# Attention numerators as full 128-row products, with tokens tiled in global pairs

## The chip, the cores and the metric

The kernel runs on one core of a Trainium2 chip. The metric is the device time of one execution in microseconds (us); lower is better. The core's engines are TensorE (PE in the profile, with its weight loads as PEld), VectorE (DVE), ScalarE (ACT), GpSimd (POOL) and SyncE (SP); SP and POOL only start DMA transfers here, apart from a few set-up instructions.

## The reference

Linear attention with cosine weights, followed by a gated feed-forward block (FFN). There are 8 batches, 8 heads, 576 tokens and head size 64; the FFN has model width 512 and inner width 1536.

```python
pos = np.arange(S); theta = np.pi / 2.0 * pos / S
phi(x) = concat([max(x, 0) * cos(theta), max(x, 0) * sin(theta)], -1)
kv  = einsum('bhsf,bhsd->bhfd', phi(k), v)
z   = sum(phi(k), axis=2)
num = einsum('bhsf,bhfd->bhsd', phi(q), kv)
den = einsum('bhsf,bhf->bhs', phi(q), z)[..., None] + 1e-06
x   = (num / den).transpose(0, 2, 1, 3).reshape(B * S, H * D)   # 4608 x 512
out = (silu(x @ w_gate) * (x @ w_val)) @ w_out
```

## The kernel before

**Layout.** The 576 tokens of a batch are cut into NC = 9 chunks of 64 tokens (chunk c holds the tokens 9p + c). Heads are numbered 2g + e; a head's partitions are the half e, and g = 0 to 3 is split into j = g // 2 and i = g % 2. In the transposed queries `qt` the partitions are (i, head dimension), so that 128 partitions hold two heads of 64 rows each.

**Attention of one batch.** `relu_k` (line 166) takes max(k, 0), `vmul` (line 176) multiplies v by the cosine and the sine table, and a 65th column of the table itself gives the denominator. `kv_mm` (line 203) forms the 64 x 130 matrices of all heads in two PSUM banks (cosine part w = 0, sine part w = 1, 65 columns each), and `kv_out` (line 219) copies them to SBUF as `kvs`. The queries are turned by `qturn_pe` (line 194, TensorE transposes, batches 0 and 1) or by `relu_q` and `qturn_dma` (lines 171 and 188, a DMA transpose started by SP, batches 2 to 7).

**The half.** `a_half` (line 242) makes the numerators of four heads for one tile of two chunks: four products with 64 contraction rows each (line 250) into two banks,

```python
lhsT=qt[hs, e, j, c:c + n]                       # 64 rows x 128 tokens
rhs=kvs[hs, e, j]                                # 64 rows x 130 columns
```

then ScalarE scales the cosine part (`tmp`, line 260) and VectorE adds the scaled sine part (`num`, line 262). After both halves (j = 0, 1), `x_norm` (line 267) adds 1e-6, takes the reciprocal and multiplies (line 275, one 128 x 512 product), and `x_turn` (line 281) transposes the tile into `xT`, by TensorE and ScalarE (`fast`) or by a DMA transpose that SP starts (line 295). Tiles never cross a batch or a group of 8 chunks (`tiles_of`, line 232), so each batch has five tiles, one of them with a single chunk: 80 halves in all.

**FFN.** A group is 8 chunks, 512 tokens; there are NTG = 9 groups (0 to 8). `ffn_fc` (line 300) does one of the FC = 12 column blocks: four products for the gate and four for the value (line 312), SiLU on ScalarE (`sg`, line 315), product on VectorE (`ht`, line 317). `ffn_out` (line 322) does one of the group's four output tiles in 12 products (line 329), copies it out of PSUM and writes it with two DMAs (line 344).

**What sets the order.** The schedule is manual: each engine runs its instructions in the order in which the program writes them. PSUM's 8 banks go round in turn (`take`, line 66): a request for two gets the next aligned pair, and banks that are held (the two of `kv_mm`, the output tiles in progress) are skipped. An instruction that gets a bank waits until its last reader is through. From group 1 on, a group is SLOTS = 16 slots, 12 column blocks and 4 output tiles; slot s of group g is 16g + s. After each, the functions that the table `plan` holds for that slot are issued. For batch b from 3 on, `kv_mm` is at slots 1 and 2 of group b - 1, and the ten halves at slots 4 to 13. For batch 2, `relu_q`, `relu_k` and `vmul` are at slots 17 to 20, `qturn_dma` at 20, `kv_mm` at 23 and 24 and the halves at 26 to 35; `qturn_dma` of batch 3 is at 29. Group 2 begins at slot 32. Its first token pair comes from batch 1, the next three from batch 2, the last of them at slots 30 and 31.

Group 0 is special. Its column blocks run in two passes over 256 tokens each, called the a pieces (first 256) and b pieces here; six a pieces come first, with the halves and transposes of tiles 2 and 3 between them (`early`, line 453), then b and a pieces alternate. Its output tiles are done in three pieces of four products for all four tiles (line 470), which holds four banks, with work for batch 1 between them (`sub`, line 411).

Of the kernel before, what the change touches and what calls it, by code (L numbers as in the profile page):

```python
# [9 lines left out]
FP32 = mybir.dt.float32  # L10
# [7 lines left out]
def kernel(  # L18
# [86 lines left out]
    CA = 4  # L105
    load(0, "v", 2)
    load_slots(0, "q", 0, CA)
    load_slots(0, "q", CA, NC)
# [3 lines left out]
    bias = consts.tile([P, 2, 2], FP32)  # L112
    for i, step in enumerate((S, S - 1)):
# [8 lines left out]
    for i, cs in enumerate((csk, cst)):  # L122
        nc.scalar.activation(out=cs[:, :, 0], in_=pos, func=AF.Sin, scale=-rad, bias=bias[:, i, 0:1])
        nc.scalar.activation(out=cs[:, :, 1], in_=pos, func=AF.Sin, scale=rad, bias=bias[:, i, 1:2])
# [94 lines left out]
    def kv_out(b, engs=("act",)):  # L219
        kvs = kvp.tile([P, 2, J, 2 * D1], BF16, name="kvs")  # L220
        ps = st.pop((b, "kvps"))
        held.pop(("kv", b))
        n = 2 // len(engs)
        for i, eng in enumerate(engs):
            es = slice(i * n, (i + 1) * n)
            (nc.scalar.copy if eng == "act" else nc.vector.tensor_copy)(
                out=kvs[:, es].rearrange("p e j x -> p e (j x)"), in_=ps[:, es, 0:J * 2 * D1])
        st[b, "kvs"] = kvs
# [3 lines left out]
    def tiles_of(b):  # L232
        cut = next((g - b * NC for g in range(0, NH + 1, GH) if b * NC < g < (b + 1) * NC), NC)
        res = []
        for lo, hi in ((0, cut), (cut, NC)):
            while lo < hi:
                n = min(2, hi - lo)
                res.append((lo, n))
                lo += n
        return res  # L240

    def a_half(b, c, n, j):

        m = n * SH
        qt, kvs = st[b, "qt"], st[b, "kvs"]
        av = take(2)[0:m, :, 0:4 * D1].rearrange("p i (w e x) -> p i w e x", w=2, e=2)
        for e in range(2):
            for i in range(2):
                hs = slice(i * D, (i + 1) * D)
                nc.tensor.matmul(  # L250
                    out=av[:, i, :, e],
                    lhsT=qt[hs, e, j, c:c + n].rearrange("p c s -> p (c s)"),
                    rhs=kvs[hs, e, j].rearrange("p (w x) -> p w x", w=2),
                    start=True, stop=True,
                )
        if j == 0:
            st[b, "num", c] = smp.tile([P, H, D1], FP32, name="num")
        nv = st[b, "num", c][0:m, 4 * j:4 * j + 4].rearrange("p (i e) x -> p i (e x)", i=2)
        tmp = smp.tile([P, 2, 2 * D1], FP32, name="tmp")
        nc.scalar.activation(out=tmp[0:m], in_=av[:, :, 0].rearrange("p i e x -> p i (e x)"),  # L260
                             func=AF.Copy, scale=cst[0:m, c, 0:1])
        nc.vector.scalar_tensor_tensor(  # L262
            out=nv, in0=av[:, :, 1].rearrange("p i e x -> p i (e x)"), scalar=cst[0:m, c, 1:2], in1=tmp[0:m],
# [3 lines left out]
    def x_norm(b, c, n):  # L267
        m = n * SH
        num = st.pop((b, "num", c))
        den = smp.tile([P, H, 1], FP32, name="den")  # L270
        nc.vector.tensor_single_scalar(out=den[0:m], in_=num[0:m, :, D:D1], scalar=1e-6, op=ALU.add)
        rec = smp.tile([P, H, 1], FP32, name="rec")
        nc.vector.reciprocal(out=rec[0:m], in_=den[0:m])  # L273
        x = xp.tile([P, d_model], BF16, name="x")
        nc.vector.tensor_tensor(  # L275
            out=x[0:m].rearrange("p (h d) -> p h d", h=H),
            in0=num[0:m, :, 0:D], in1=rec[0:m].to_broadcast([m, H, D]), op=ALU.mult,
        )
        st[b, "x", c] = x

    def x_turn(b, c, n, fast=False):
        m = n * SH
        x = st.pop((b, "x", c))
# [235 lines left out]
```

## Time and profile before

| What | Value |
|---|---|
| Median of 3 runs | 363.44 us (363.05 to 364.62) |
| The profiled execution's own time | 362.56 us |
| Its span, first to last instruction | 360.4 us |
| TensorE busy | 329.9 us, 92% of the span |
| VectorE busy | 189.0 us, 52% |
| ScalarE busy | 157.2 us, 44% |
| Line 250, the products of the halves | 320 products, 23.1 us |

The span is what the trace covers; the time of that execution is 2.16 us longer. Busy times of one engine can overlap in the rows of products, since they are pipelined: the start times of successive rows say more than their lengths. An engine's idle time counts only where it delays the chain of work that ends last.

### The profile page before, as it was taken

The page shows a single profiled execution, that of the slowest core. Times are in us where ns is not written, and L with a number is a line of the kernel's source. Part 1 is how long each engine was busy: PE and PEld are TensorE (multiplying, and loading weights), DVE is VectorE, ACT ScalarE, POOL GpSimd, SP SyncE. Part 2 cuts the span into 40 slices and gives each one's busy share as a digit, 9 for nine tenths or more (in the row PEclk, how much of TensorE's full clock was granted, in tenths as well). Part 3 has the DMA queues.
Part 4 walks back from the last instruction along what each step waited for, and adds up shares of the span by engine and source line. Part 5 has one row for each costly group of instructions (what it writes and reads, how often), then busy time and mean ns, then how long its engine had stood idle before and what let it go on. Part 6 is the DMA issues. An engine that isn't in the chain of part 4 may idle for free.

```text
span 360.4 us, 6121 instructions
## 1 busy us (share of the span) xinstructions
PE 329.9 (92%) x2400; PEld 154.0 (43%) x2400; DVE 189.0 (52%) x386; ACT 157.2 (44%) x301; POOL 33.3 (9%) x49
## 2 busy tenths in 40 slices
PE   0678999699956999999999999999999999999994
PEld 0447754244422444444344444444443444444441
DVE  5645753583651787438733874387337544303420
ACT  4544455483721674257425742574245323313311
POOL 8545210002000200020000000000000000000000
PEclk9879999999996999999999999999999999999999
DMA  8999999941962594649460145015501240031013
GB/s 214 196 200 202 206 208 208 256 75 18 217 136 52 88 165 74 144 68 162 81 139 1 25 86 135 6 31 90 129 1 25 57 105 0 1 74 45 0 31 87
DMA packets 56477, 36.39 MB, mean 101 GB/s; under 512 B 30848, under 2 KB 51328, under 8 KB 56448
## 3 DMA queue, kind: packets, MB, share of 16 engines
q0 software_dynamic: 21152, 18.29, 32.1%
q1 hardware_dynamic: 35296, 17.70, 23.2%
q8 instruction: 19, 0.31, 0.4%
q14 instruction: 10, 0.08, 0.1%
HBM read 37.75 MB, written 9.44 MB: 131 GB/s over the span
## 4 chain that ended last, share of the span: by engine, by line
PE 87%; DVE 4%; DMA 3%; SPq 2%; ACT 2%; issue 1%; POOL 0%; ACTq 0%; POOLq 0%
PE banks L312 53%; PE banks L329 25%; PE banks L250 5%; PE banks L212 3%; DMA raw_q<-in_q_dram 2%; DVE x L275 2%; DVE num L262 1%; SPq L189 1%; SPq L344 1%; PE banks L291 1%; PE banks L198 1%; DMA xT<-x 1%; ACT tmp L260 1%; DVE rec L273 0%; ACT xT L293 0%
## 5 line engine op out<-in xcount | busy, mean ns | idle before, releaser
L317 DVE TENSOR_TENSOR ht<-sg,banks 128x512 bf16<-128x512 bf16 (+1 forms) x120 | 75.7, 632 | 98.8 <-PE banks L312 82.7
L312 PE MATMUL banks<-xT,wg_sb 128*128 128x512 bf16 (+1 forms) x480 | 115.3, 363 | 8.8 <-DMA xT<-x 7.0
L312 PE MATMUL banks<-xT,wv_sb 128*128 128x512 bf16 (+1 forms) x480 | 114.5, 361 | 0.0
L315 ACT ACTIVATE sg<-banks 128x512 bf16<-128x512 f32 (+1 forms) x120 | 66.5, 554 | 94.2 <-PE banks L312 93.7
L329 PE MATMUL banks<-wo_sb,ht 128*128 128x512 bf16 x432 | 98.9, 380 | 0.0
L312 PEld LDWEIGHTS <-wv_sb 128*128 128x128 bf16 x480 | 47.5, 99 | 47.5 <-issue 1.1
L312 PEld LDWEIGHTS <-wg_sb 128*128 128x128 bf16 x480 | 42.2, 98 | 49.5 <-DMA xT<-x 7.2
L329 PEld LDWEIGHTS <-ht 128*128 128x128 bf16 x432 | 39.8, 98 | 46.7
L260 ACT ACTIVATE tmp<-banks,cst 128x260 f32<-128x260 f32 (+1 forms) x80 | 37.8, 477 | 42.4 <-PE banks L250 42.4
L262 DVE SCALAR_TENSOR_TENSOR num<-banks,cst,tmp 128x260 f32<-128x260 f32 (+1 forms) x80 | 38.5, 483 | 15.7 <-ACT tmp L260 15.2
L341 DVE COPY ob<-banks 128x512 f32<-128x512 f32 x17 | 11.8, 691 | 37.7 <-PE banks L329 36.2
L275 DVE TENSOR_TENSOR x<-num,rec 128x512 bf16<-128x512 f32 (+1 forms) x40 | 27.6, 690 | 1.4
L341 ACT COPY ob<-banks 128x512 f32<-128x512 f32 x18 | 10.5, 586 | 39.9 <-PE banks L329 39.9
L250 PE MATMUL banks<-kvs,qt 64*128 64x130 bf16 (+1 forms) x320 | 23.1, 227 | 1.1 <-ACT ob L341 0.7
L177 DVE TENSOR_TENSOR v<-raw_v,tab 128x1152 bf16<-128x1152 bf16 x32 | 23.5, 751 | 0.7 <-DMA raw_v<-in_v_dram 0.7
L250 PEld LDWEIGHTS <-qt 64*128 64x128 bf16 (+1 forms) x320 | 9.7, 96 | 32.8 <-issue 30.9
L212 PE MATMUL banks<-v,raw_k 64*64 64x130 bf16 x576 | 12.9, 231 | 8.6 <-DVE v L177 8.6
L212 PEld LDWEIGHTS <-raw_k 64*64 64x64 bf16 x576 | 10.0, 113 | 13.6 <-issue 8.0
L162 ACT ACTIVATE raw_k<-raw_k 128x576 bf16<-128x576 bf16 x24 | 15.8, 675 | 0.0
L162 ACT ACTIVATE r_q<-raw_q 128x576 bf16<-128x576 bf16 x24 | 15.8, 673 | 0.0
L93 POOL DMA_DIRECT2D raw_k<-in_k_dram x7 | 5.2, 743 | 99.9 <-issue 59.3
L291 PE MATMUL banks<-ident,x 128*128 128x128 bf16 (+1 forms) x40 | 4.2, 232 | 6.3 <-DVE x L275 6.3
(38 smaller groups left out, 77.1 us busy)
## 6 DMA issues: line engine op xcount, KB each, us to landing
out_dram<-ob SPq DMA_DIRECT2D x72, 128.0 KB, 2.3
raw_k<-in_k_dram POOLq DMA_DIRECT2D x7, 576.0 KB, 13.0
raw_v<-in_v_dram POOLq DMA_DIRECT2D x6, 576.0 KB, 12.8
raw_q<-in_q_dram POOLq DMA_DIRECT2D x6, 576.0 KB, 12.2
wg_sb<-in_moe_w_gate_dram POOLq DMA_DIRECT2D x6, 256.0 KB, 10.8
wv_sb<-in_moe_w_val_dram POOLq DMA_DIRECT2D x6, 256.0 KB, 11.1
wo_sb<-in_moe_w_out_dram POOLq DMA_DIRECT2D x3, 512.0 KB, 13.0
k<-in_k_dram SPq DMA_DIRECT2D x2, 576.0 KB, 4.2
```

The costliest lines, as they stand in the source:

```text
L162: nc.scalar.activation(out=out, in_=in_, func=AF.Relu)
L177: nc.vector.tensor_tensor(out=v2s[b % 2][:, g, :, :, 0:D], in0=raws[b, "v"][:, g].unsqueeze(2).to_broadcast([P, NC, 2, D]), in1=tab, op=AL ...
L212: nc.tensor.matmul(out=ps[i * D:(i + 1) * D, e, j * 2 * D1:(j + 1) * 2 * D1], lhsT=raws[b, "k"][es, g, c], rhs=v2s[b % 2][es, g, c, :, 0:D ...
L250: nc.tensor.matmul(out=av[:, i, :, e], lhsT=qt[hs, e, j, c:c + n].rearrange("p c s -> p (c s)"), rhs=kvs[hs, e, j].rearrange("p (w x) -> p ...
L260: nc.scalar.activation(out=tmp[0:m], in_=av[:, :, 0].rearrange("p i e x -> p i (e x)"), func=AF.Copy, scale=cst[0:m, c, 0:1])
L262: nc.vector.scalar_tensor_tensor(out=nv, in0=av[:, :, 1].rearrange("p i e x -> p i (e x)"), scalar=cst[0:m, c, 1:2], in1=tmp[0:m], op0=ALU ...
L275: nc.vector.tensor_tensor(out=x[0:m].rearrange("p (h d) -> p h d", h=H), in0=num[0:m, :, 0:D], in1=rec[0:m].to_broadcast([m, H, D]), op=AL ...
L312: nc.tensor.matmul(out=o, lhsT=w[:, kc, fs], rhs=xT[tg][:, kc, ts], start=(kc == 0), stop=(kc == KC - 1))
L315: nc.scalar.activation(out=sg[:, 0:n], in_=ps[0], func=AF.Silu)
L317: nc.vector.tensor_tensor(out=ht[:, fc, r:r + n], in0=sg[:, 0:n], in1=ps[1], op=ALU.mult)
L329: nc.tensor.matmul(out=o_ps[t], lhsT=ht[:, fc, r:r + P], rhs=wo_sb[:, fc], start=(fc == 0), stop=(fc == FC - 1))
L341: (nc.scalar.copy if t % 2 == 0 else nc.vector.tensor_copy)(out=ob, in_=ps)
```

## The change

- `kvs` is replaced by two constant tiles `kvd`, cleared once. `kv_out` writes the two heads of a pair (i = 0, 1) as two copies, one for each half of the partitions and into its own columns, so that a pair's matrices stand on a block diagonal of 128 rows x 260 columns.
- `a_half(t, j)` takes a global tile t = 0 to 35 (chunks 2t and 2t + 1 of the 72). It does two products of 128 rows x 260 columns in place of four of 64 x 130. Tiles 4, 13, 22 and 31 cross from one batch to the next; each of their products is done as two, with 64 tokens each. There are 72 halves.
- `x_norm` multiplies in two products of 128 x 256.
- The tables are written anew: one half per slot. A group's four tiles are at slots 4 to 11 of the group before (group 2's at 20, 21, 23 to 28). Batch 2's key and query work is at slots 16 to 19, its `qturn_dma` at 20, its `kv_mm` at 20 and 21; batch 3's `qturn_dma` is split over 28 and 29. In group 0, tile 2 is issued ahead of the FFN, and the tiles of batch 1 are spread anew.
- The weights' fifth part is loaded ahead of batch 1's keys, and the loads of batches 4 to 7 are issued at three places in the program each.

The diff, cut (constants for the cosine of the ninth chunk, the load order and the unchanged ends of functions left out):

```diff
+    kvd = []
+    for j in range(2):
+        t = consts.tile([P, 2, J, 2, 2, D1], BF16, name=f"kvd_{j}")
+        nc.vector.memset(t, 0.0)
+        kvd.append(t)
...
-    def kv_out(b, engs=("act",)):
-        kvs = kvp.tile([P, 2, J, 2 * D1], BF16, name="kvs")
+    def kv_out(b, engs=("act", "act")):
...
+            hs = slice(i * D, (i + 1) * D)
             (nc.scalar.copy if eng == "act" else nc.vector.tensor_copy)(
-                out=kvs[:, es].rearrange("p e j x -> p e (j x)"), in_=ps[:, es, 0:J * 2 * D1])
+                out=kvd[b % 2][hs, :, :, :, i].rearrange("p e j w x -> p e (j w) x"),
+                in_=ps[hs, :, 0:J * 2 * D1].rearrange("p e (y x) -> p e y x", x=D1))
...
-                    out=av[:, i, :, e],
-                    lhsT=qt[hs, e, j, c:c + n].rearrange("p c s -> p (c s)"),
-                    rhs=kvs[hs, e, j].rearrange("p (w x) -> p w x", w=2),
+                    out=ps[ms, e, 0:4 * D1],
+                    lhsT=st[b, "qt"][:, e, j, c:c + n].rearrange("p c s -> p (c s)"),
+                    rhs=kvd[b % 2][:, e, j].rearrange("p w i x -> p (w i x)"),
...
+    x_turn(0, fast=True)
+    a_(2, 0)()
+    x_turn(1, fast=True)
+    a_(2, 1)()
...
+    at("a0", a_(3, 0))
+    at("a1", a_(3, 1))
+    at("a3", turn(2, True))
+    at("a5", turn(3, True))
...
+    at((0, 0), a_(5, 0), q_(1, 0, 1))
+    at((0, 1), a_(5, 1), q_(1, 1, 1))
+    at((0, 2), turn(4, True), a_(6, 0))
+    at((0, 3), a_(6, 1))
+    at((1, 0), turn(5, True), a_(7, 0))
+    at((1, 1), a_(7, 1))
...
+        keng = "dve" if b == 2 else "act"
+        steps = [lambda b=b, g=g: (relu_k(b, g, g + 1, keng), vmul(b, g)) for g in range(G)]
...
+            fs, tq, tk = [s0 + i // 2 for i in range(8)], (s0 + 4, s0 + 4), (s0 + 4, s0 + 5)
...
+    for t in range(2 * OUT, NTG * OUT):
+        tg, i = divmod(t, OUT)
+        s = SLOTS * (tg - 1) + (4 if tg > 2 or i == 0 else 5) + 2 * i
+        at(s, a_(t, 0))
+        at(s + 1, a_(t, 1), turn(t))
```

How the instructions move, at three places. First SP around the start of group 2; `xT_1053` is group 2's input before and `xT_1120` in the change. Before:

```order
L189 DMA_TRANSPOSE qt_1080<-r_q_1009 128x18x64 x2
L295 DMA_TRANSPOSE xT_1053<-x_1256 128x4x128
L344 DMA out_0_dram<-ob_1273 64x512 x2
L344 DMA out_0_dram<-ob_1301 64x512 x2
L295 DMA_TRANSPOSE xT_1053<-x_1316 128x4x128
L189 DMA_TRANSPOSE qt_1329<-r_q_1231 128x18x64 x2
L344 DMA out_0_dram<-ob_1344 64x512 x2
L344 DMA out_0_dram<-ob_1368 64x512 x2
L295 DMA_TRANSPOSE xT_1053<-x_1383 128x4x128
```

Of the change:

```order
L195 DMA_TRANSPOSE qt_1010<-r_q_955 128x18x64 x2
L290 DMA_TRANSPOSE xT_1120<-x_1117 128x4x128
L290 DMA_TRANSPOSE xT_1120<-x_1176 128x4x128
L290 DMA_TRANSPOSE xT_1120<-x_1219 128x4x128
L339 DMA out_0_dram<-ob_1253 64x512 x2
L195 DMA_TRANSPOSE qt_1257<-r_q_1165 128x18x64
L290 DMA_TRANSPOSE xT_1120<-x_1268 128x4x128
L339 DMA out_0_dram<-ob_1284 64x512 x2
L195 DMA_TRANSPOSE qt_1257<-r_q_1165 128x18x64
L339 DMA out_0_dram<-ob_1301 64x512 x2
```

Group 2's last input tile stood behind the output writes of all four tiles of group 1; it now stands behind those of the first, and behind one of batch 3's two query transposes.

Second VectorE at the start of group 0, from the second tile's `den` on (`ht` is the first FFN result). Before:

```order
L271 TENSOR_SCALAR den_302<-num_291 128x8
L273 RECIPROCAL rec_304<-den_302 128x8
L275 TENSOR_TENSOR x_306<-num_291,rec_304 128x512
L317 TENSOR_TENSOR ht_135<-sg_349,banks_90 128x256
L262 SCALAR_TENSOR_TENSOR num_356<-banks_90,cst_114,tmp_357 128x260
L317 TENSOR_TENSOR ht_135<-sg_368,banks_90 128x256
L262 SCALAR_TENSOR_TENSOR num_356<-banks_90,cst_114,tmp_375 128x260
L271 TENSOR_SCALAR den_378<-num_356 128x8
L273 RECIPROCAL rec_380<-den_378 128x8
L275 TENSOR_TENSOR x_382<-num_356,rec_380 128x512
```

Of the change:

```order
L265 TENSOR_SCALAR den_304<-num_295 128x8
L267 RECIPROCAL rec_306<-den_304 128x8
L271 TENSOR_TENSOR x_308<-num_295,rec_306 128x2x2x64 x2
L257 SCALAR_TENSOR_TENSOR num_341<-banks_90,cst_118,tmp_342 128x260
L257 SCALAR_TENSOR_TENSOR num_341<-banks_90,cst_118,tmp_352 128x260
L265 TENSOR_SCALAR den_355<-num_341 128x8
L267 RECIPROCAL rec_357<-den_355 128x8
L271 TENSOR_TENSOR x_359<-num_341,rec_357 128x2x2x64 x2
L312 TENSOR_TENSOR ht_145<-sg_370,banks_90 128x256
L257 SCALAR_TENSOR_TENSOR num_375<-banks_90,cst_118,tmp_376 128x260
L312 TENSOR_TENSOR ht_145<-sg_387,banks_90 128x256
```

The third tile's `num`, `den`, `rec` and `x` stood between and behind the first two `ht`; they are now ahead of them.

Third ScalarE at the first column blocks of group 1, where batch 2's keys and queries are prepared. Before:

```order
L315 ACTIVATE sg_987<-banks_90 128x512
L260 ACTIVATE tmp_995<-banks_90,cst_114 128x260
L315 ACTIVATE sg_1006<-banks_90 128x512
L162 ACTIVATE r_q_1009<-raw_q_163 128x9x64 x2
L260 ACTIVATE tmp_1016<-banks_90,cst_114 128x260
L315 ACTIVATE sg_1033<-banks_90 128x512
```

Of the change:

```order
L310 ACTIVATE sg_950<-banks_90 128x512
L168 ACTIVATE raw_k_169<-raw_k_169 128x576
L168 ACTIVATE r_q_955<-raw_q_173 128x9x64
L310 ACTIVATE sg_965<-banks_90 128x512
L168 ACTIVATE raw_k_169<-raw_k_169 128x576
L168 ACTIVATE r_q_955<-raw_q_173 128x9x64
```

Each of the first four slots now has one key step and one query step on ScalarE, and the halves of batch 1's last tile have moved out of the first two.

## Rows read from the trace of the kernel before

**Rows 1.** The profile's page: TensorE's busy time, its granted clock in 40 slices.

```profile
PE 329.9 (92%) x2400; PEld 154.0 (43%) x2400; DVE 189.0 (52%) x386; ACT 157.2 (44%) x301; POOL 33.3 (9%) x49
...
PEclk9879999999996999999999999999999999999999
```

**Rows 2.** Waits of TensorE: who waited for whom; us in total, times, longest.

```profile
PE banks L312 <- DMA xT<-x: 7.0, 1, 7.0
PE banks L291 <- DVE x L275: 6.3, 7, 1.9
```

**Rows 3.** Timeline, group 1's end, TensorE and VectorE: start us, length us, engine, line.

```profile
103.81 0.29 PE L250 MATMUL banks<-kvs,qt 64*128 64x130 bf16 x4
105.62 0.69 DVE L275 TENSOR_TENSOR x<-num,rec 128x512 bf16<-128x512 f32 x1
```

**Rows 4.** The chain that ended last, entry of group 2: start us, length us, what.

```profile
108.62 2.45 DMA xT<-x
...
111.12 3.58 PE banks L312 x8
```

**Rows 5.** The same chain in group 4, and in the last two groups.

```profile
200.29 1.83 PE banks L312 x8
202.12 0.23 PE banks L250 x4
...
293.53 20.72 PE banks L312 x96
314.25 10.36 PE banks L329 x48
```

**Rows 6.** Timeline of TensorE, a half and a full-height transpose between output products.

```profile
54.49 0.29 PE L250 MATMUL banks<-kvs,qt 64*128 64x130 bf16 x4
54.71 1.04 PE L329 MATMUL banks<-wo_sb,ht 128*128 128x512 bf16 x4
55.59 0.39 PE L291 MATMUL banks<-ident,x 128*128 128x128 bf16 x4
55.81 1.03 PE L329 MATMUL banks<-wo_sb,ht 128*128 128x512 bf16 x4
```

**Rows 7.** Timeline of TensorE, the marks of group 0; idle time before, and its end.

```profile
19.07 1.01 PE L312 MATMUL banks<-xT,wg_sb 128*128 128x256 bf16 x4 [0.67 <-ACT xT L293]
...
30.30 0.60 PE L312 MATMUL banks<-xT,wg_sb 128*128 128x256 bf16 x4 [0.67 <-ACT xT L293]
...
49.94 1.04 PE L329 MATMUL banks<-wo_sb,ht 128*128 128x512 bf16 x4
...
68.59 1.02 PE L312 MATMUL banks<-xT,wg_sb 128*128 128x512 bf16 x4 [0.46 <-ACT xT L293]
```

**Rows 8.** Timeline of VectorE at the start, with its waits for loads.

```profile
5.91 0.76 DVE L164 TENSOR_SCALAR raw_k<-k 128x1152 bf16<-128x1152 f32 x1 [0.67 <-DMA k<-in_k_dram]
7.39 2.84 DVE L177 TENSOR_TENSOR v<-raw_v,tab 128x1152 bf16<-128x1152 bf16 x4 [0.72 <-DMA raw_v<-in_v_dram]
```

**Rows 9.** Groups of instructions by line and form: busy us, mean ns, idle before.

```profile
L317 DVE TENSOR_TENSOR ht<-sg,banks 128x512 bf16<-128x512 bf16 x96 | 65.8, 685 | 84.9 <-PE banks L312 82.7 <-PE banks L250 1.1 <-ACT sg L315 1.1
L262 DVE SCALAR_TENSOR_TENSOR num<-banks,cst,tmp 128x260 f32<-128x260 f32 x64 | 30.9, 485 | 13.7 <-ACT tmp L260 13.4
L177 DVE TENSOR_TENSOR v<-raw_v,tab 128x1152 bf16<-128x1152 bf16 x32 | 23.5, 751 | 0.7 <-DMA raw_v<-in_v_dram 0.7
L275 DVE TENSOR_TENSOR x<-num,rec 128x512 bf16<-128x512 f32 x32 | 22.1, 692 | 1.1
L226 ACT CAST kvs<-banks 128x520 bf16<-128x520 f32 x7 | 4.1, 592 | 5.0 <-PE banks L212 4.9
L317 DVE TENSOR_TENSOR ht<-sg,banks 128x256 bf16<-128x256 bf16 x24 | 9.9, 418 | 13.8 <-ACT sg L315 13.8
L128 DVE CAST tab<-csk 128x1152 f16<-128x1152 f32 x1 | 1.0, 976 | 1.1 <-ACT csk L124 1.1
```

**Rows 10.** DMA transposes of the queries (line 189): time from issue to landing.

```profile
DMA to landing us min/median/max: 4.0/4.4/4.9
```

More of the change, by code (lines that the diff above doesn't have):

```diff
@@ L230, with a_half @@
     xT = {}
[L232 to L246, printed above, removed]
-        for e in range(2):
-            for i in range(2):
-                hs = slice(i * D, (i + 1) * D)
+    def a_half(t, j):
+        (b0, c0), (b1, c1) = (divmod(2 * t + r, NC) for r in range(2))
+        ps = take(2)
+        for e in range(2):
+            if b0 == b1:
+                parts = [(slice(0, P), b0, c0, 2)]
+            else:
+                parts = [(slice(0, SH), b0, c0, 1), (slice(SH, P), b1, c1, 1)]
+            for ms, b, c, n in parts:
@@ L344, in ffn_out, with at, slot, a_ @@
             nc.sync.dma_start(out=out_v[idx // NC, idx % NC], in_=ob[e * SH:(e + 1) * SH])
-    def load_next(b):
-        if b < B:
-            for nm in ("k", "v", "q"):
-                load(b, nm)
-    for i in range(4):
+    for i in range(5):
         load_w(i)
     load(1, "k")
-    load_w(4)
+    load(1, "v", 2)
     load_w(5)
-    load(1, "v", 2)
-    load_slots(1, "q", 0, CA)
+    load_slots(1, "q", 0, CUT[1])
     for i in range(3):
         load_wo(i)
-    load_slots(1, "q", CA, NC)
-    load_next(2)
+    load_slots(1, "q", CUT[1], NC)
+    for nm in ("k", "v", "q"):
+        load(2, nm)
+    OUT = GH // 2
+    SLOTS = FC + OUT
+    plan = {}
+    def at(s, *fns):
+        plan.setdefault(s, []).extend(fns)
+    def slot(s):
+        for f in plan.pop(s, ()):
+            f()
+    def a_(t, j):
+        return lambda: (a_half(t, j), x_norm(t) if j else None)
+    def turn(t, fast=False):
+        return lambda: x_turn(t, fast)
+    def q_(b, j, part):
+        lo, hi = ((0, CUT[b]), (CUT[b], NC))[part]
+        return lambda: qturn_pe(b, j, lo, hi, "act")
     for i in range(2):
@@ L370 @@
     vmul(0, 2)
[L371 removed]
+    q_(0, 0, 0)()
     vmul(0, 3)
[L373 removed]
     kv_mm(0, 1)
     kv_out(0, ("act", "dve"))
[L376 removed]
+    q_(0, 1, 0)()
     for t in range(2):
[L378 to L388 removed]
@@ L408 @@
-    at(10, lambda: (kv_mm(1, 1), kv_out(1)))
-    at(11, lambda: qturn_pe(1, 1, 0, CA, "act"))
-    sub = {}
-    halves = [(c, n, j) for c, n in ts1 for j in range(J)]
-    for i, (c, n, j) in enumerate(halves[:4]):
-        sub[0, i] = [lambda c=c, n=n, j=j: a_half(1, c, n, j)]
-        if j:
-            sub[0, i].append(lambda c=c, n=n: x_norm(1, c, n))
-    sub[1, 0] = [lambda: x_turn(1, *ts1[0], fast=True)]
-    sub[1, 1] = [lambda: x_turn(1, *ts1[1], fast=True)]
-    sub[1, 2] = [lambda: qturn_pe(1, 0, CA, NC, "act")]
@@ new lines @@
+    at("a9", lambda: relu_k(1, 2, 4, "dve"))
+    for g in range(G):
+        at(f"b{4 + g}", lambda g=g: vmul(1, g))
+    at("a10", lambda: kv_mm(1, 0))
+    at("a11", lambda: kv_mm(1, 1), lambda: kv_out(1, ("act", "dve")))
+    at("b9", q_(1, 0, 0))
+    at("b10", q_(1, 1, 0), a_(4, 0))
+    at("b11", a_(4, 1))
+    at((0, 0), a_(5, 0), q_(1, 0, 1))
[3 more added lines that the diff above has]
+    at((1, 0), turn(5, True), a_(7, 0))
@@ L470 @@
+    at((1, 1), a_(7, 1))
+    at((1, 2), turn(6, True))
+    at((2, 0), turn(7, True))
+    HALF = GH // 2
+    for nm, f in order:
+        ffn_fc(0, f, *((0, HALF) if nm == "a" else (HALF, GH)))
+        slot(f"{nm}{f}")
     for piece in range(3):
```

181 lines of the change are left out of this document (66 added, 115 removed).

## The prediction

> **What bounds the kernel now.** I read the page first: TensorE is busy for 92% of the span, so time is won by taking work off TensorE or by closing its gaps [rows 1]. Its granted clock is full except for a fall in slices 2 and 3 (about 9 to 27 us) and a smaller one in slice 13 (about 108 to 117 us), each behind idle TensorE. Then the list of TensorE's waits: behind the one for the first data there is a single 7.0 us wait of line 312 for an `xT` transpose, and 6.3 us in seven waits of `x_turn` for `x` [rows 2]. Then the chain of waits. It runs through TensorE nearly all the way; the place where it leaves is the entry of group 2. There batch 2's third tile is made at slots 30 and 31: its last half starts at 103.81, `x` is ready at 105.62 + 0.69 = 106.31 [rows 3], SP is busy with earlier issues until 108.62, the tile lands at 111.07, and the next eight products take 3.58 us [rows 4]. From group 3 on the chain shows no wait at all.
>
> So there are two kinds of stretch. Groups 3 to 8 are pure TensorE work: the last two, without attention, take 20.72 + 10.36 = 31.08 us each, 1.73 us for a column block (20.72 / 12) and 2.59 for an output tile (10.36 / 4) [rows 5]. Groups 0 to 2 carry the waits.
>
> **What one half costs.** With a half behind it, a column block and the half take 1.83 + 0.23 = 2.06 us [rows 5], 0.33 more than a block alone. Only 0.23 of that lies between the half's first product and the next block; another 0.10 passes before the half can begin. The transposes of `x_turn` are a control: they are full 128 x 128 products, come in fours of 128 columns, and fit in with no such gap. They start 0.88 us after an output piece began whose four products take 0.86, and last 0.22 [rows 6], 55 ns per 128 columns. I therefore take the extra 0.10, and a like part of the 0.23, as the price of going to 64-row products and back. A half of the change is two full-height products of 260 columns: 2 x 260 / 128 x 55 ns = 0.22 us, and no gap. In the four tiles that cross batches the products are 64 tokens wide again; there I take the 0.22 and two gaps of 0.11, 0.44.
>
> The Trainium skill says so too, and the opposite as well (TensorEngine Tiling (Array Packing)). Key Properties: changing the tiling mode drains TensorE; by that rule the sum below stands. Theoretical Speedup: a dimension of 64 or less allows up to twofold tiling; by that rule alone the zero blocks of the change double the streamed columns, a half costs more than now (0.44 with the gaps kept), and term 1 below would be a loss of 4.1 in place of a gain of 6.9. The transposes' rows [rows 6] agree with the drain.
>
> No row separates streaming from the gap inside the 0.23, so the dearer half is the first rival.
>
> **The change part by part**, against the profiled execution's own 362.56 us.
>
> 1. *Halves in groups 1 to 8.* Before there are 62 (two of batch 1's last tile, ten for each of six batches): 62 x 0.33 = 20.5 us. Now 28 tiles, 56 halves, 6 of them crossing: 50 x 0.22 + 6 x 0.44 = 13.6. Gain **6.9**. Bounds: nothing if the gaps stay, 8.2 if crossing costs nothing extra. `kv_mm` is unchanged.
>
> 2. *Entry of group 2.* The last tile now ends at slot 28, with three output tiles (3 x 2.59 = 7.8 us) and the half itself (0.22) ahead of group 2. From the half to the landed `xT` it took 111.07 - 103.81 = 7.3 us before, SP's queue included [rows 3, 4]; a split `x` adds some 0.15. So it lands about half a us ahead of its use. The wait of 7.0 goes [rows 2], and the first eight products return from 3.58 to 1.73 since TensorE doesn't idle ahead of them: gain 7.0 + 1.85 = **8.9**. Bounds: 8.9, and 6 if the query transpose ahead of it on SP holds it up by a us or two. What is late next is `qt` of batch 2: its halves start at slot 23, 3 slots behind `qturn_dma`, where before they started at 26.
>
> 3. *Front of group 0*, first FFN product to first b piece: 30.30 - 19.07 = 11.2 us now [rows 7]. Tile 2 moves ahead of the FFN, into time in which TensorE waits for tile 1's `xT` anyway. Left are six pieces of 0.87 (two of them at half clock, as now: 6.9 together), two halves and two transposes (1.1), and the wait for the last `xT` copy (0.7): 8.7, gain 2.5. The two clearings of `kvd` stand on VectorE ahead of the first max(k, 0). The nearest row is the table copy, 976 ns for 1152 elements, so 0.88 each, 1.8 together [rows 9]; VectorE waits there for loads now, 0.67 and 0.72 [rows 8], so 0 to 0.4 comes through; I take 0.3. Start of the FFN otherwise unchanged: `kv_out`'s copies of 520 columns take 592 ns where half of them did before, but `kv_mm` of j = 1 no longer stands behind the second query turn. Gain **2.2**. By the Trainium skill (VectorE: DVE Perf Modes, Zero memsets can be issued as uint32) a memset takes a cycle per element; the estimate from it would be 1.1 us each, and 0.8 late.
>
> 4. *b pieces of group 0*, 49.94 - 30.30 = 19.6 us now [rows 7]: 18 pieces (15.7), `kv_mm` (1.5), query turns (1.0) and tile 4's crossing halves (0.9) make 19.1. Gain **0.5**. The moved loads have cover: batch 1's keys are used some 4 us behind their landing by the loads' order and rate.
>
> 5. *Output pieces of group 0*, 68.59 - 49.94 = 18.65 us now [rows 7]. Twelve pieces 10.4, six halves 1.3, four transposes 0.9, two query turns 0.9. The waits for `x` at its end go, since the last turn is now three pieces ahead of the end. In their place comes a wait for banks: four are held, and following `take`, five halves in a row (tile 5's second to tile 7's second) get the same pair, so each waits until VectorE has read the one before, behind the `x_norm` of the tile before that. I get two waits of 0.6. Sum 14.7, gain **4.0**; bounds 2 and 5.
>
> 6. *New wait in group 1.* Following `take` again, the block at slot 22 asks for the two banks of batch 2's `kv_mm`, which ended at slot 21 only 0.22 us earlier; `kv_out`'s two copies on ScalarE are 2 x 0.592 us [rows 9]. Loss **1.0** (0.9 to 2, if ScalarE is late). Batch 2's max(k, 0) adds to that: `keng` is read when the slot runs, and by then the loop has left it at "act", so it stays on ScalarE although "dve" is written. The three load places change nothing: for batches 3 to 7 POOL has the same order and waits for the same buffers.
>
> 7. *Nothing on the path:* the later groups' table. A group's last tile ends at slot 11, four output tiles (10.4 us) ahead of its use; that is the cover. SP has 28 `xT` transposes in place of 30.
>
> Sum: 6.9 + 8.9 + 2.2 + 0.5 + 4.0 - 1.0 = 21.5, so 341.1. The profiled execution lies 0.9 under the median of the runs shown, so I forecast **342.0 us**.
>
> **The rivals.**
>
> *The half's price isn't the gap.* If each detour keeps its fixed part and only the streaming doubles, a half costs 0.33 to 0.44. At 0.44, 50 halves in groups 1 to 8 and about 12 in group 0 lose 0.22 each: 342 + 13.6 = 355.6; at 0.33, 349. For it: nothing in the rows shows a 64-row product without its gaps. Against it: the transposes in [rows 6].
>
> *Batch 2's queries are late.* The first transpose of `qt` starts after ScalarE's last `relu_q`, about 8.7 us into group 1 (four blocks, 6.9 us, and about 1.8 that ScalarE is behind); with the second's issue and 4.4 to land [rows 10] that is some 15 us, against a first use at 16.8. Loads still run there in the change; if they double the landing, TensorE waits 2 to 4 us and may lose clock as in [rows 4], another 1.9: 344 to 348. The entry of group 2 can add a us or two.
>
> *Group 0 keeps its length*, since another chain (loads, the low clock) sets it: 342 + 6 = 348.
>
> *VectorE becomes the bound*, and the kernel is slower. In slots 4 to 11 it has eight `ht` (0.685), eight `num` (0.485), three `vmul` (0.751) and four `x_norm` [rows 9]. An `x_norm` is two short operations (0.4) and two products; by `ht`'s 418 ns for 256 columns these are 0.42 each. That sums to 5.5 + 3.9 + 2.3 + 5.0 = 16.7 us, against TensorE's 8 x 1.95 = 15.6: just over, and the eight banks and the output tiles cover about 2 us. If the split products took 0.69 each, as the undivided one does now, the stretch would be 18.8 and cost about 1.3 us in each of seven groups: 351. It takes over 0.9 us each, 3.1 us per group, to pass 363; the decision lies there.
>
> **How the numbers follow.** Forecast as described 0.65 (338 to 346); late queries or entry 0.15 (344 to 350); gap kept 0.08 (349 to 356); group 0 unchanged 0.06 (346 to 350); VectorE bound 0.04, of which half over 363; anything else 0.02. The range of 8 in 10 runs from 337.5 (crossing free, no bank waits, no offset to the median) to 350. A measurement of this kernel can tell about 0.5%, 1.8 us, from no change. Faster by more 0.95, within 0.02, slower by more 0.03.
>
> **What would show it.** Group starts in the chain: group 1 at about 62 us in place of 68.59, groups 3 to 6 about 34.4 us apart where they were 35.9, group 7 32.9. The products of the halves 0.22 apart with the next block right behind. No wait of line 307 for `xT`, and full clock in slice 13. A wait of about 1 us of TensorE for `kvd`'s copies in group 1, and two of about 0.6 for `num` between the output pieces. I am wrong if a half still takes 0.33, if the entry wait reappears at slot 23 or 32, or if VectorE shows no idle time in slots 4 to 11 while TensorE waits for it.

## The result and the profile after

The median of the changed kernel is **341.26 us** (four runs, 340.19 to 341.92) against 363.28 us of the kernel before beside it: ratio 0.938, 95% interval 0.935 to 0.942. The forecast was 342.0 us, with a range of 337.5 to 350. The profiled execution took 340.19 us, with a span of 338.4, so 22.0 less span than before.

The page, lines as in [rows 1]:

```profile
PE 320.1 (95%) x2232; PEld 162.7 (48%) x2232; DVE 185.3 (55%) x409; ACT 157.3 (46%) x299; POOL 32.8 (10%) x49
...
PEclk9999999999999999999999999999999999999999
```

TensorE is busy for 9.8 us less and the rest of the gain is idle time that went. The waits of TensorE that answer to [rows 2], leaving out the one for the first data:

```profile
PE banks L307 <- ACT xT L288: 1.2, 2, 0.7
PE banks L307 <- ACT kvd L230: 1.0, 1, 1.0
PE banks L246 <- DVE num L257: 0.9, 2, 0.5
PE banks L246 <- DVE kvd L230: 0.9, 1, 0.9
PE banks L287 <- DVE x L271: 0.7, 1, 0.7
```

The 7.0 us for `xT` by DMA and six of the seven waits for `x` are gone. New are three that the prediction had named (line 307 for `kvd`, twice line 246 for `num`) and one that it had not: the first half of the program, on line 246, waits for `kvd` from VectorE.

The timeline of TensorE, marks of group 0 as in [rows 7], and the start of group 1:

```profile
19.71 0.60 PE L307 MATMUL banks<-xT,wg_sb 128*128 128x256 bf16 x4 [0.45 <-ACT xT L288]
...
27.01 0.60 PE L307 MATMUL banks<-xT,wg_sb 128*128 128x256 bf16 x4 [0.72 <-ACT xT L288]
...
45.91 1.04 PE L324 MATMUL banks<-wo_sb,ht 128*128 128x512 bf16 x4
...
60.77 1.03 PE L307 MATMUL banks<-xT,wg_sb 128*128 128x512 bf16 x4
```

And the chain that ended last, around the start of group 2 (the 16 products at 96.43) and its first halves, where before [rows 4] and [rows 5] stood:

```profile
89.95 6.47 PE banks L324 x30
96.43 3.45 PE banks L307 x16
```

```profile
106.58 0.22 PE banks L246 x2
106.80 1.73 PE banks L307 x8
108.52 0.22 PE banks L246 x2
108.75 1.73 PE banks L307 x8
110.47 0.34 PE banks L246 x4
110.81 1.83 PE banks L307 x8
112.65 0.34 PE banks L246 x4
```

Group 2 begins right behind the last output tile. A full half takes 0.22 and the block behind it starts at once; a crossing half takes 0.34 and makes the block behind it 0.10 longer, so 0.44.

| Stretch | Before | Forecast | After |
|---|---|---|---|
| first FFN product | 19.07 | 19.4 | 19.71 |
| to first b piece | 11.23 | 8.7 | 7.30 |
| to first output piece | 19.64 | 19.1 | 18.90 |
| to group 1 | 18.65 | 14.7 | 14.86 |
| group 1 to the end of the span | 291.8 | 277.0 | 277.6 |

The columns before and after add up to their spans (360.4 and 338.4). Groups 3 to 6 start 35.91 apart before, and 34.82 or 34.36 after, as a crossing tile is among the four or not.

### The profile page after: what moved, and what is told of

The parts are those of the page before. It is cut to its first block, busy times and chain, and to the rows that moved or that the text cites. A ratio compares the mean times of both kernels' runs of the same rounds, so it can differ in the third digit from the quotient of the medians.

```text
span 338.4 us, 5797 instructions
## 1 busy us (share of the span) xinstructions
PE 320.1 (95%) x2232; PEld 162.7 (48%) x2232; DVE 185.3 (55%) x409; ACT 157.3 (46%) x299; POOL 32.8 (10%) x49
## 4 chain that ended last, share of the span: by engine, by line
PE 91%; DVE 5%; ACT 2%; issue 1%; ACTq 0%
PE banks L307 55%; PE banks L324 27%; PE banks L246 5%; PE banks L218 3%; DVE num L257 1%; DVE x L271 1%; PE banks L204 1%; ACT tmp L256 1%; DVE kvd L143 1%; DVE v L183 0%; ACT L124 0%; ACT kvd L230 0%; PE banks L287 0%; DVE raw_k L170 0%; DVE tab L129 0%
## 5 line engine op out<-in xcount | busy, mean ns | idle before, releaser
L307 PE MATMUL banks<-xT,wg_sb 128*128 128x512 bf16 (+1 forms) x480 | 113.1, 358 | 2.3 <-ACT xT L288 1.2
L324 PE MATMUL banks<-wo_sb,ht 128*128 128x512 bf16 x432 | 96.2, 379 | 0.0
L324 PEld LDWEIGHTS <-ht 128*128 128x128 bf16 x432 | 41.8, 98 | 47.9 <-issue 0.4
L307 PEld LDWEIGHTS <-wg_sb 128*128 128x128 bf16 x480 | 45.4, 98 | 39.1 <-issue 4.1
L256 ACT ACTIVATE tmp<-banks,cst 128x260 f32<-128x260 f32 x72 | 34.1, 476 | 14.8 <-PE banks L246 14.6
L257 DVE SCALAR_TENSOR_TENSOR num<-banks,cst,tmp 128x260 f32<-128x260 f32 x72 | 34.7, 484 | 10.0 <-ACT tmp L256 9.7
L246 PE MATMUL banks<-kvd,qt 128*128 128x260 bf16 (+1 forms) x160 | 28.5, 285 | 1.8 <-DVE num L257 0.9
L271 DVE TENSOR_TENSOR x<-num,rec 128x256 bf16<-128x256 f32 x72 | 27.4, 421 | 1.2
L246 PEld LDWEIGHTS <-qt 128*128 128x128 bf16 (+1 forms) x160 | 13.8, 102 | 18.2 <-issue 5.4
L230 ACT CAST kvd<-banks 64x520 bf16<-64x520 f32 x14 | 8.3, 594 | 6.1 <-PE banks L218 6.0
## 6 DMA issues: line engine op xcount, KB each, us to landing
raw_q<-in_q_dram POOLq DMA_DIRECT2D x6, 576.0 KB, 15.2
```

Source lines behind the costliest of these rows:

```text
L246: nc.tensor.matmul(out=ps[ms, e, 0:4 * D1], lhsT=st[b, "qt"][:, e, j, c:c + n].rearrange("p c s -> p (c s)"), rhs=kvd[b % 2][:, e, j].rear ...
L256: nc.scalar.activation(out=tmp, in_=av[:, :, 0], func=AF.Copy, scale=cst[:, c0, 0:1])
L257: nc.vector.scalar_tensor_tensor(out=st["num", t][:, j], in0=av[:, :, 1], scalar=cst[:, c0, 1:2], in1=tmp, op0=ALU.mult, op1=ALU.add,)
L271: nc.vector.tensor_tensor(out=x[:, 4 * j * D:(4 * j + 4) * D].rearrange("p (i e d) -> p e i d", i=2, e=2), in0=num[:, hs, 0:D].rearrange(" ...
L307: nc.tensor.matmul(out=o, lhsT=w[:, kc, fs], rhs=xT[tg][:, kc, ts], start=(kc == 0), stop=(kc == KC - 1))
L324: nc.tensor.matmul(out=o_ps[t], lhsT=ht[:, fc, r:r + P], rhs=wo_sb[:, fc], start=(fc == 0), stop=(fc == FC - 1))
```

## The experiments

Each run's time goes with a ratio to the kernel before on its own chip, and a gain below is that ratio's share of 363.3 us. Two changed kernels are compared by their medians; as the kernel before itself has medians from 363.28 to 365.23 on the chips used, such a difference is also read in place. For beside the times, the distances between the starts of groups 3 to 7 repeat to 0.02 us in every kernel as long as the groups hold the same work, so the price of a half can be read from them. A group without attention takes 31.08 [rows 5]; two `kv_mm` pieces of 0.65, each with 0.10 more on the block behind it, make 1.50. What is left over 32.58 is halves. Group 7 of the changed kernel is a test of it: it has eight halves and no `kv_mm`, and its 32.85 less 31.08 gives the same 0.22. All of the table is worked out so, and it is where the halves of the runs are read:

| Kernel | Groups apart | Halves in it | One half |
|---|---|---|---|
| before | 35.91 | 10 of 64 rows, alone | 0.33 |
| after | 34.36 | 8 of 128 rows | 0.22 |
| after, with a crossing tile | 34.82 | 6 of 128 rows, 2 crossing | crossing 0.45 |
| first run (128 rows in before) | 35.26 | 8 of 128 rows, 2 single-chunk | single-chunk 0.45 |
| second run (64 rows in after) | 35.23 | 8 of 64 rows, alone | 0.33 |

**Full 128-row products in the kernel before.** The edits of `kv_out`, `a_half`, `x_norm` (two products) and the clearings from the change's diff, with the old tiles and tables.

```diff
+                out=ps[0:m, e, 0:4 * D1],
+                lhsT=st[b, "qt"][:, e, j, c:c + n].rearrange("p c s -> p (c s)"),
+                rhs=kvd[b % 2][:, e, j].rearrange("p w i x -> p (w i x)"),
```

> The kernel before with one part of the change alone: a half as two products of 128 rows x 260 columns on the block diagonal, the two copies of kv_out and the two clearings it needs. Tiles, tables and loads stay as before. Theory (the price is the gap at going to 64-row products and back): the 62 halves of groups 1 to 8 cost 62 x 0.33 = 20.5 us before; now 48 of full tiles cost 0.22 and 14 of the single-chunk tiles, whose products are 64 tokens wide, keep the gap at 0.33, 15.2 together. Gain 5.3 there and up to 1.5 from the 18 halves of group 0, less 0.3 for the clearings: 356 to 358.5 us. In the trace a half and the column block behind it take 1.95, not 2.06. Rival (the price is the streamed columns, so the zero blocks double it): a half costs 0.44, 62 x 0.11 = 6.8 us lost, 368 to 371. The entry of group 2 keeps its 7 us wait under both.

Measured: 361.41 us, ratio 0.992 (0.989 to 0.995), a gain of 2.8 where 5 to 7 were expected. The chain in group 3 shows both kinds of half:

```profile
172.93 0.22 PE banks L251 x2
173.15 1.73 PE banks L315 x8
174.88 0.22 PE banks L251 x2
175.10 2.59 PE banks L332 x12
177.69 0.34 PE banks L251 x2
178.03 2.70 PE banks L332 x12
180.73 0.34 PE banks L251 x2
```

The direction is the theory's: a full half fell from 0.33 to 0.22. But the single-chunk halves, whose products are 64 tokens wide, cost 0.34 and 0.10 on the work behind, 0.45 in place of the expected 0.33: they stream 260 columns and still pay for the detour. Eight gains and two losses of 0.11 leave 0.65 per group. So the larger products alone are worth little with the old tiles; the global pairs give the other half of the gain. Besides, the front was later: the FFN starts at 21.19 where it was 19.07 (0.79 of it was there at the first product of `kv_mm`), and here too the first half waits for `kvd` (1.4 us).

**64-row products in the changed kernel.**

```diff
+                for i in range(2):
+                    hs = slice(i * D, (i + 1) * D)
...
+                        lhsT=st[b, "qt"][hs, e, j, c:c + n].rearrange("p c s -> p (c s)"),
+                        rhs=kvd[b % 2][hs, e, j, :, i],
```

> The changed kernel with one part undone: a half is again four products of 64 rows x 130 columns (of the crossing tiles eight, with 64 tokens each). Tiles, tables, loads and the copies of kv_out stay as in the change. Theory (the gap): 50 halves of groups 1 to 8 go from 0.22 back to 0.33, 5.5 us, the six crossing ones from 0.44 to 0.44 to 0.66, up to 1.3, and group 0 adds up to 1: 346.5 to 349 us. Rival (the streamed columns): half the columns cost half of 0.22, so 0.11 less for each of 62 halves, 334 to 336.

Measured: 346.71 us, ratio 0.952 (0.949 to 0.955), 5.4 us over the changed kernel, of which 4.6 lie behind the start of group 1 (282.2 us to the end where it was 277.6), as the gap has it; the rival is refuted by 11 us. The chain in group 3:

```profile
146.27 0.22 PE banks L248 x4
146.49 1.83 PE banks L308 x8
148.32 0.22 PE banks L248 x4
```

A half and its block take 2.05 again. Half the columns, and 0.11 dearer.

**The entry of group 2 alone, in the kernel before.**

```diff
-            2: (s0 + 1, 2, s0 + 4, s0 + 7, 1),
+            2: (s0 + 1, 2, s0 + 4, s0 + 7, 2),
```

> The kernel before with one number of its table altered: batch 2's halves two per slot, at slots 26 to 30, so that group 2's last token pair is made by slot 28 in place of 31 and its transpose stands ahead of three output tiles. Theory: the 7.0 us wait at the entry of group 2 and the 1.85 us of slow first products behind it go: 363.3 - 8.9 = 354.4 (354 to 357.5, if the query transpose ahead on SP keeps up to 3 us of it). Rival (SP's queue, not the late half, sets when the tile lands): the wait stays at 4 us or more, 359 or over.

Measured: 355.23 us, ratio 0.976 (0.971 to 0.980), a gain of 8.9. No wait for `xT` by DMA is left. The chain at the end of group 1 shows the entry (108.47) and what nobody had asked for:

```profile
102.73 2.70 PE banks L329 x12
105.43 0.35 PE banks L250 x8
105.78 2.70 PE banks L329 x12
108.47 1.73 PE banks L312 x8
```

Two halves in a row (x8) take 0.35 and 0.10 behind, 0.45 together, where one alone takes 0.33. The part that doubles is 0.12, the part that does not is 0.21. The gain therefore also holds about 1 us from batch 2's five pairs; against that, in the profiled execution the granted clock was low at the start of group 1 (0.79 over 60 to 75 us), where the first two blocks took 3.57 and 2.75 us in place of 1.89 and 1.83.

**Both together.**

> The edits of the first and the third run together: full 128-row products and batch 2's halves two per slot in the kernel before. Theory: the two gains lie in different places of the one chain and add up, 5 to 6.5 and 8.9: 347.5 to 350 us. What is then left to the changed kernel's 341.3 is group 0 (3.92 + 0.74 + 3.79 - 0.64 = 7.8 us in the two traces). Rival (one of them frees the chain for another chain): they don't add up, 351 or more.

Measured: 352.28 us, ratio 0.967 (0.962 to 0.972), a gain of 12.2 where the two alone gave 2.8 and 8.9: they add up. The time itself lies where the rival put it, but not for the rival's reason: the first run had shown the products to be worth 2.8 here and not 5 to 6.5, for the single-chunk halves and the later front.

What is left to the changed kernel lies mostly in group 0, and no run takes its new order alone. The runs together still tell what it hangs on. From the first FFN product to group 1 the five profiles of kernels with the old tables take 49.1 to 50.0 us, the eight with the new ones 41.1 to 42.3, whichever products they have (49.10 in the first run, with the new products; 41.84 in the second, with the old). So the new order (tiles, tables and loads together) gains some 8 us there, and the shape of the products next to nothing.

**The changed kernel again, and three small edits beside it.** First the yardstick:

> The changed kernel once more, as the yardstick for the three small edits beside it on the same chip: 341.3 us within 1 us, a wait of 1.0 us for kvd in group 1, two of 0.4 to 0.5 for num between group 0's output pieces, and kv_out's second copy of batch 0 on VectorE starting only when the one on ScalarE has ended.

Measured: 341.44 us, ratio 0.935 (0.932 to 0.938). All of the expected waits are there, but the front ran differently. Stretches of the timeline, with TensorE's busy time and, third from the end, its granted clock: first the profiled execution of the changed kernel, then this one:

```profile
19.70:23.00 3.30, 3.17 (x28) 2.68 (x28) 2.82 (x9) 1.84 (x5) 2.10 (x3) 1.00 1.45 196
```

```profile
19.50:23.00 3.50, 3.50 (x20) 2.57 (x20) 2.54 (x7) 1.18 (x3) 2.11 (x3) 0.60 1.45 197
```

Here the clock was at its lower level for most of the first two a pieces, and from the FFN's first product to the first b piece it took 8.37 us and not 7.30. The two executions of this one program ran alike up to the first half (13.34 and 13.33), but not from there. The halves of the first two tiles, first in the changed kernel's profile, then here:

```profile
13.34 1.89 PE L246 MATMUL banks<-kvd,qt 128*128 128x260 bf16 x8 [0.87 <-DVE kvd L230]
```

```profile
13.33 1.05 PE L246 MATMUL banks<-kvd,qt 128*128 128x260 bf16 x8 [1.00 <-DVE kvd L230]
```

The first took about twice as long for them, as at the lower level (the row of the granted clock has 1.00 for 13.3 to 19.7 there; the products' lengths say otherwise). So the first execution had its slow stretch ahead of the FFN, where it cost 0.22 (first half to first FFN product 6.37 and 6.16), and this one behind, where it cost 1.07.

*The hold on batch 2's banks.*

```diff
+        if b != 2:
+            held.pop(("kv", b))
...
+            at(s0 + 6, lambda: held.pop(("kv", 2)))
```

> The changed kernel with one line moved: the two banks of batch 2's kv_mm are given back to the rotation one slot later, so that the column block of slot 22 takes another pair. Theory (the wait at slot 22 is for kv_out's two copies and for nothing else): the 0.98 us wait of line 307 for kvd goes, 1.0 us less than the changed kernel. Rival (batch 2's queries are next): TensorE waits at slot 23 for their landing instead, since it gets there 1 us earlier, and the time stays. In the trace of the changed kernel the queries' issue is at 68.78 and their use at 77.67, so I expect no such wait.

Measured: 340.12 us, ratio 0.932, 1.3 below the yardstick. The wait is gone; the block of slot 22 follows its half at once, and group 2 starts 34.36 behind group 1 where it was 35.49:

```profile
73.99 0.39 PE L247 MATMUL banks<-kvd,qt 128*128 128x260 bf16 x2
74.22 1.03 PE L308 MATMUL banks<-xT,wg_sb 128*128 128x512 bf16 x4
```

In the changed kernel the same place reads

```profile
72.85 0.39 PE L246 MATMUL banks<-kvd,qt 128*128 128x260 bf16 x2
72.97 1.20 ACT L230 CAST kvd<-banks 64x520 bf16<-64x520 f32 x2 [0.87 <-PE banks L218]
...
74.22 1.02 PE L307 MATMUL banks<-xT,wg_sb 128*128 128x512 bf16 x4 [0.98 <-ACT kvd L230]
```

so the wait was the length of `kv_out`'s two copies, 1.20, and nothing else: ScalarE had been idle for 0.87 when they began.

*Four output banks in a row.*

```diff
+            if t == 0:
+                take(4)
+                for u in range(4):
+                    held["o", u] = [bank_at[0] - 4 + u]
```

> The changed kernel with the four banks of group 0's output tiles taken as one aligned run of four, so that the halves between the output pieces go round two pairs and not one. Theory (the waits of 0.49 and 0.39 us of line 246 for num come from five halves in a row on one pair of banks): both go, and the marks from 45.91 to 60.77 shorten by up to 0.9 us, or by less where the input of a half is late too. Rival (VectorE itself is late with num there): the waits stay in sum, on another pair.

Measured: 341.28 us, ratio 0.934 (0.930 to 0.938). The time can't be told from the yardstick's, since in its profile the first product of `kv_mm` came 0.76 later. In place it is as expected: the output pieces take 14.07 us and not 14.87, with one wait of 0.25 left.

```profile
50.88 0.38 PE L246 MATMUL banks<-kvd,qt 128*128 128x260 bf16 x2 [0.25 <-DVE num L257]
```

*`kv_out` by banks.*

```diff
+            if "dve" in engs:
+                for n in range(2):
+                    hs = slice(n * D, (n + 1) * D)
...
+                        out=kvd[b % 2][hs, i, :, :, n].rearrange("p j w x -> p (j w) x"),
+                        in_=ps[hs, i, 0:J * 2 * D1].rearrange("p (y x) -> p y x", x=D1))
+                continue
```

> The changed kernel with kv_out of batches 0 and 1 as four copies of 64 rows x 260 columns, two for each bank: those of the first bank on ScalarE, those of the second on VectorE. Theory (the second copy starts at 12.58, when the first has ended at 12.55, because both read the same two banks): the two engines now run side by side, and the first half starts 0.3 to 0.6 us earlier than 13.34; the time falls by as much, 0.1%. Rival (VectorE is late for another reason, its vmul): the start of the first half doesn't move, or is later, since four copies cost more than two.

Measured: 341.68 us, ratio 0.935 (0.932 to 0.939): no difference in time. The timeline of the changed kernel shows the two copies one behind the other, and that of this run side by side:

```profile
11.95 0.60 ACT L230 CAST kvd<-banks 64x520 bf16<-64x520 f32 x1 [0.54 <-PE banks L218]
...
12.58 0.70 DVE L230 CAST kvd<-banks 64x520 bf16<-64x520 f32 x1 [2.37 <-ACT kvd L230]
...
13.34 1.89 PE L246 MATMUL banks<-kvd,qt 128*128 128x260 bf16 x8 [0.87 <-DVE kvd L230]
```

```profile
12.99 0.76 ACT L233 CAST kvd<-banks 64x260 bf16<-64x260 f32 x2 [0.52 <-PE banks L218]
13.03 0.87 DVE L233 CAST kvd<-banks 64x260 bf16<-64x260 f32 x2 [1.81 <-PE banks L218]
...
13.81 0.38 PE L253 MATMUL banks<-kvd,qt 128*128 128x260 bf16 x1 [0.29 <-ACT kvd L233]
```

From the copies' start to the first half it takes 0.82 in place of 1.39. That the shared banks are the reason is the plain reading, but the edit also parts the columns of `kvd` that the two copies write, so the run doesn't tell the two apart. Of the 0.57 only 0.20 arrives: from the first product of `kv_mm` to the first FFN product it took 11.25 and not 11.45 (in both profiles the first halves ran at the lower clock). In the time even that is not seen: the first product of `kv_mm` came 0.98 later in this execution, and at slot 23 a half waited 0.79 for batch 2's second query transpose, the rival "late queries" of the prediction. The transposes took 8.0 us to land here, 7.6 in the changed kernel's profile and 6.3 in its repeat, where no half waited for them; so there is little margin.

**All of them, and crossing tiles in one slot.** Beside the three edits:

```diff
-        at(s, a_(t, 0))
+        at(s + (t % 9 == 4), a_(t, 0))
```

> A version meant to beat the changed kernel: the three small edits together (the hold at slot 22, the four output banks, kv_out by banks), and from group 2 on the two halves of a crossing tile in one slot, so that TensorE goes to 64-token products and back once per tile and not twice. Expected against the changed kernel's 341.4: the wait at slot 22, -1.0; the output pieces, -0.8; the front, -0.5; three crossing tiles at 0.22 each, -0.7. Sum -3.0: 338.4. If batch 2's queries land too late for slot 23 (one run showed 0.8 us of it), 339 to 340. Rival (each gain is passed on to the next wait): 341 or more.

Measured: 339.88 us, ratio 0.930 (0.928 to 0.932), about 1.5 us below the changed kernel and half of what was hoped. It is the lowest median of all, but can't be told from the 340.12 of the later release alone. Each edit pays in its place: group 1 takes 34.73 and not 35.50 (with a wait of 0.2 for queries), groups with a crossing tile 34.59 and not 34.82, the output pieces 14.07. The rest is lost to the front of the profiled execution, where the first product of `kv_mm` came 0.63 later and the stretch to the first b piece took 8.68 with a low clock.

**x_norm's products twice, in the changed kernel.**

```diff
+            if t >= 8:
+                nc.vector.tensor_tensor(
...
```

> The changed kernel with x_norm's two products issued twice for the tiles from the 8th on (the second writes the same values), 0.76 us more of VectorE for each tile, 3.0 us per group in slots 4 to 11. It tests the cover that the prediction gave VectorE there. Theory (cover of about 2 us): in the trace of the changed kernel VectorE works without a pause for some 11 us in a group and just comes up with TensorE at its end, so 1 to 2 us of TensorE waiting for num, sg or ht appear in each of seven groups: 348 to 356 us. Rival (the cover is deeper, since the output tiles at slot 12 need no VectorE result at once): within 1 us of the changed kernel, 340.5 to 342.5.

Measured: 344.25 us, ratio 0.942 (0.941 to 0.944), 2.9 over the changed kernel and below what the theory had. Groups 2 to 5 last 35.13 each, 0.31 or 0.77 more than there, group 1 0.9 more, and groups 6 and 7, which have no `vmul`, no more. The wait is one for `ht`; in group 3:

```profile
155.38 1.02 PE L313 MATMUL banks<-xT,wv_sb 128*128 128x512 bf16 x4 [0.55 <-DVE ht L318]
```

The two more products took 0.93 us of each tile's time on VectorE (1.60 for the four where the two take 0.67), more than the expected 0.76. So of 3.7 us more VectorE work per group at most 0.9 reaches TensorE. Groups 2 to 5 all last the same 35.13, with a crossing tile or without: VectorE sets their length now. The edge is near, but the cover is deeper than the 2 us of the prediction.

**Old products, two halves per slot.** The kernel before, with 64-row products:

```diff
-            s = tk + J + 1 + i // hn
+            s = tk + J + 1 + i // 2 * (1 if b == 2 else 2)
```

> The kernel before with its 64-row products kept, and the two halves of a tile issued in one slot, batch 2's at slots 26 to 30 and those of the later batches in every other slot. It asks whether the price of 64-row products belongs to the half or to the detour. Theory (to the detour: in the third run two halves in one slot took 2.18 - 1.73 = 0.45 us together, where one alone takes 0.33): 25 pairs save 0.21 each beside the 8.9 us of the entry, 363.3 - 8.9 - 5.3 = 349.1, no worse than the full 128-row products with the same entry (351 to 352). Rival (the price comes with each half): the entry's gain alone, 354.4; or more than that, if two halves in a row make VectorE late for the banks.

Measured: 351.32 us, ratio 0.961 (0.959 to 0.963), against 0.967 (0.962 to 0.972) for full products with the same entry. The timeline of TensorE in group 3:

```profile
150.61 0.41 PE L250 MATMUL banks<-kvs,qt 64*128 64x130 bf16 x8
...
154.51 0.41 PE L250 MATMUL banks<-kvs,qt 64*128 64x130 bf16 x8
...
167.13 0.39 PE L329 MATMUL banks<-wo_sb,ht 128*128 128x512 bf16 x1 [0.20 <-DVE ht L317]
```

A pair and two blocks take 3.90, less 2 x 1.73 is 0.44 for two halves: the price belongs to the detour. The groups are 35.21 apart, 0.70 less than before, where 1.05 was expected; 0.20 of the rest is the wait above, VectorE being late by the second half of the slot. Group 6 bears this out: it has the halves but no `vmul`, TensorE waits for nothing in it, and it takes 34.84, the whole 1.07 less. With that the old products, merely paired, are as good as the full ones on the old tiles (35.21 against 35.26 between groups).

## Why the prediction was right, and where it was not

1. *Halves in groups 1 to 8.* Right in mechanism and size: 0.22 and 0.44 forecast, 0.22 and 0.45 found. Sharper now: a lone 64-row half is 0.11 of streaming and 0.22 of detour. The half that the prediction read (behind 200.29 in [rows 5]) is one of a single chunk, 64 tokens; those of full tiles in the same group, at 195.94 and 198.00, take the same 0.22 to 0.23, so the price stands. The weight loads (PEld) show where the fixed part lies. A half of each kernel, before and after:

```profile
195.87 0.11 PEld L250 LDWEIGHTS <-qt 64*128 64x128 bf16 x4 [0.42 <-issue]
195.87 0.29 PE L250 MATMUL banks<-kvs,qt 64*128 64x130 bf16 x4
```

```profile
148.81 0.31 PEld L246 LDWEIGHTS <-qt 128*128 128x128 bf16 x2
149.03 0.39 PE L246 MATMUL banks<-kvd,qt 128*128 128x260 bf16 x2
```

Among full products the weights are loaded 0.22 ahead of their first product, under the one before it. The 64-row weights are loaded only as their own products begin, after 0.42 of idle time, and so are the block's weights at the return (196.09, its first product at 196.10). That fits a pause at either change of shape, about as long as one load (0.10); no row shows what TensorE does in it. The rule of the Trainium skill that speaks of doubled work (TensorEngine Tiling (Array Packing), Theoretical Speedup) holds too, in the pair, where four 64-row products of 130 columns add only 0.11 to 0.12. But the other rule of the Trainium skill decides here (the same page, Key Properties, switching drains), because each detour carried one half; the trace agrees with it as far as these loads go. The first rival, that the half's price is not the gap, fell in the second run.

2. *Entry of group 2.* Right in mechanism, and near in size: group 2 follows the output tile. The run with that alone gained 8.9, of which about 1 is its pairs. In the changed kernel this term and the halves were to give 15.8 behind the start of group 1; with the 1.0 of slot 22 added back, the traces have 14.2 + 1.0 = 15.2.

3. *Front of group 0.* Two misses of opposite sign. The first FFN product was forecast 0.3 later; it came 0.64 later in the profiled execution and 0.42 in the repeat, the other 0.22 being the lower clock of the first halves. The step that failed is "Start of the FFN otherwise unchanged": `kv_out`'s copies were taken by their duration (592 ns) and not by their order. The second waits for a semaphore of the first; with the copies side by side the FFN's start came 0.20 nearer. The two products of `x_norm` were left out of this term too: 0.76 to 0.77 us where the one took 0.69 to 0.70, for each of the two tiles on this path. The clearings were sized right (925 ns each, 0.88 forecast; the other estimate, 1.1, was too long), and came through with 0.08 us, VectorE's `vmul` starting at 7.47 in place of 7.39. The forecast of 8.7 for the first stretch counted two pieces at half clock. The profiled execution had none and took 7.30; the repeat had them and took 8.37, near the forecast. So how near this term comes is luck of the execution.

4. *b pieces:* 18.90 for 19.1.

5. *Output pieces:* 14.86 for 14.7. The two bank waits were 0.49 and 0.39, not 0.6, and the edit of the four banks showed them to be the banks' order. The rival "group 0 keeps its length" is out: the order shortened it in every profile with the new tables.

6. *Slot 22:* 0.98 for 1.0, and removing its cause gave the time back. The addition that batch 2's max(k, 0) on ScalarE makes it longer was wrong: ScalarE was idle.

7. *Nothing on the path:* right, with more reserve on VectorE than the 2 us given. By the sum of the rival "VectorE becomes the bound", 3.7 us more per group would cost 16.7 + 3.7 - 15.6 - 2.0 = 2.8; it cost 0.3 to 0.9.

One reading was off, without weight for the sum: the fall of the clock in slice 13 is not the smaller one (its digit in [rows 1] is 6, those of slices 2 and 3 are 8 and 7).

What stays open: why, in the same program, the clock is low ahead of the FFN in one execution and behind its start in another. The runs show that it is, and what it costs behind (about 1.1 us of 341) and ahead (0.2). Open too is what group 0's parts are worth one by one.

## What to carry to other kernels

Where small products of another tile shape stand between large ones, price the detour and not only the columns: group them, or give them the large shape with zeros, and see that the remainder tiles don't bring the small shape back (here a single chunk at 0.45 ate a quarter of the gain of four full tiles). Read a steady stage's price from the distance of its repeats, which here held to 0.02 us while executions of one kernel scattered by 1.5 us and more. When a copy is spread over two engines, look at what both touch (here the same banks, and interleaved columns) before counting them as parallel.

## What was not expected of the hardware

The shape's detour is the same for fewer rows and for fewer tokens: 0.21 to 0.22 around four products of 64 rows x 128 tokens, and 0.23 around those of 128 rows x 64 tokens, as the last version showed by taking one of two detours out of a group (34.82 to 34.59). A crossing half with four such products costs 0.45, and a single-chunk half with two costs the same, so two 64-token products of a crossing pair cost no more together than one alone. Eight products of 64 rows and 64 tokens in a crossing half cost 0.35 with the detour, by the second run's groups of 35.27: less than the 0.45 of the full-height form. And the start of the program varies: the first product of `kv_mm` stood anywhere from 8.20 to 9.66 us in these profiles.
